# Issuing three opening loads from ScalarE behind its statistics, and spreading the loads of x, in an attention and gated-MLP kernel

## The chip, the cores and the metric

The kernel runs on one core of one Trainium2 chip. The metric is the device time of one execution in microseconds (us), lower is better. A timed execution is some 1.8 us longer than the span of its profile, which runs from the first to the last recorded instruction. A difference of 2% would be 39 us.

## The reference, cut to what matters

```python
xn  = layernorm(x)                                    # x: 2048 x 640, bfloat16
q   = xn @ wq                                         # 32 heads of 192
p   = softmax(q k_cache^T * 192**-0.5)                # 2048 keys per head
s   = (p @ v_cache, heads side by side) @ wo
g   = silu((silu(xn @ w1) * (xn @ w3)) @ w2)          # hidden size 1536
out = x + s * g
```

## The kernel before: the parts that the change touches

The kernel goes through the 32 heads, each with four blocks of 512 queries. TensorE's program is a fixed list: scores, values and projections, interleaved. The opening has to bring head 0 and query block 0 to the point where that list can run. Loads are issued by SyncE (`nc.sync`), weights by GpSimd (`nc.gpsimd`). Cut to the core:

```python
def head_start():
    load_x(0, 0, 2)              # x of query block 0, in two parts
    load_x(0, 2, 4)
    load_k0(0)                   # K of head 0, keys 0..1023 ("K half 0")
    load_w0()                    # three weight loads, issued by GpSimd
    load_k0(1)                   # K half 1
    load_x(1)                    # x of block 1 ("x1")
    load_v(0, (0,))              # V half 0
    turn_over(34)                # 34 matmuls on the identity: warm-up of TensorE
    ln_stats(0, 0)               # layernorm statistics: VectorE
    ln_stats(0, 1)
    ln_stats_act(0, 3)           # ... and ScalarE, for one tile
    ...
    turn_k0(pk0, 0, range(4))            # TensorE transposes K half 0 (16 of them)
    copy_k0(nc.scalar.copy, pk0, 0, 0)   # ScalarE copies K^T out of PSUM
    turn_over(4)
    ln_turn(0, 0, nc.scalar.copy)        # x^T, first half: TensorE, then ScalarE's copy
    turn_k0(pk1, 1, (0, 1))              # K half 1
    ln_turn(0, 1, nc.vector.tensor_copy) # x^T, second half, VectorE's copy
    ...
    load_v(0, (1,))
    for g in range(2, NQB):              # x of blocks 2 and 3
        load_x(g)
    project_first()                      # the first query projection
    ...
    ln_norm(1, 0, nc.vector)
    ln_norm(1, 1, nc.vector)
    ln_turn_dma(1, 0)                    # x^T of block 1: two DMA transposes, SyncE
    ln_turn_dma(1, 1)
    ln_stats(1, 3)
```

In the profile, L271 is the transposes of K, L391 the first query projection, L410 the second one (block 1, which needs the two DMA transposes), L569 the warm-up, `kn` the landing place of K of head 0, `W` the weights, `pst` the transposes of x.

## Time and profile before

| | before |
|---|---|
| median of the first three runs | 1942.58 us (1942.23 to 1942.89) |
| the profiled execution | 1944.41 us timed, span 1942.6 us |
| PE busy | 1930.4 us, 99% |
| idle of PE, largest | 2.8 (identity), 2.4 (K half 0), 0.7 (x^T of block 1) |

From the profile page of the kernel before: busy time, share of the span and instruction count of each engine, then the chain of work that ended last, by engine.

```profile
PE 1930.4 (99%) x27267; PEld 1319.7 (68%) x27275; DVE 654.3 (34%) x997; ACT 1180.5 (61%) x1278; POOL 282.5 (15%) x501
...
PE 98%; DMA 1%; DVE 1%; ACT 0%; issue 0%; SPq 0%; DVEq 0%; ACTq 0%
```

TensorE bounds the kernel, and only its idle time can be won. The waits of PE in the kernel before (waiting instruction and what released it: us in total, times, longest) show all of it:

```profile
PE pk L569 <- POOL ident_bf masks.py:199: 2.8, 1, 2.8
PE pk L271 <- DMA kn<-in_A_k_cache_dram: 2.4, 1, 2.4
PE ps L410 <- DMA xnT<-xn: 0.7, 1, 0.7
PE ps L391 <- ACT xnT L356: 0.3, 1, 0.3
PE st L487 <- ACT pT L490: 0.3, 1, 0.3
```

The timeline of PE in the kernel before (start in us, length in us, instruction, count, and in brackets the idle time before it with its releaser):

```profile
8.94 1.89 PE L271 MATMUL pk<-ident_bf,kn 128*128 128x128 bf16 x16 [2.35 <-DMA kn<-in_A_k_cache_dram]
...
13.54 2.34 PE L391 MATMUL ps<-xnT,W 128*128 128x256 bf16 x20 [0.31 <-ACT xnT L356]
...
29.02 2.32 PE L410 MATMUL ps<-xnT,W 128*128 128x512 bf16 x9 [0.66 <-DMA xnT<-xn]
```

K half 0 lands and PE transposes it at 8.94; 16 transposes take 1.89 us, one each 107 ns. That is half clock: in later parts of this trace the same transposes start 56 ns apart. The chain of waits gives the transfers' lengths (start, us, what): K half 0 was issued at 1.68 and took 7.21 us; the DMA transpose that released L410 was issued at 22.80 and took 6.09 us.

```profile
1.68 7.21 DMA kn<-in_A_k_cache_dram
...
22.80 6.09 DMA xnT<-xn
```

The weights' issues in the first 5 us, from the transfer view (size, us from issue to landing). They were issued at 1.30, 2.66 and 3.55, so they landed at 8.7, 11.1 and 13.0:

```profile
W<-in_A_wq_dram POOLq DMA_DIRECT2D x1, 160.0 KB, 7.4
W<-in_B_w_dram POOLq DMA_DIRECT2D x1, 80.0 KB, 8.4
W<-in_A_wq_dram POOLq DMA_DIRECT2D x1, 80.0 KB, 9.4
```

### The profile page before, as it was taken

The numbers are of one execution on the slowest core, as the hardware profiler recorded it, in microseconds if no ns is written. First come the engines' busy times: TensorE is split into PE (matmuls) and PEld (weight loads), VectorE is DVE, ScalarE is ACT, GpSimd is POOL, SyncE is SP. The second block draws the span as 40 slices with busy tenths as digits, with TensorE's granted clock in tenths as the row PEclk, the third lists the DMA queues.
The fourth block names the chain that finished last, engine by engine and source line by source line (L and its number), as shares of the span: only waits on it lengthen the run. The fifth ranks groups of instructions, "written<-read, shape, count | busy, mean of one in ns | idle before, by whom it ended". The sixth has DMA issues, their size and how long they took to land.

```text
span 1942.6 us, 59661 instructions
## 1 busy us (share of the span) xinstructions
PE 1930.4 (99%) x27267; PEld 1319.7 (68%) x27275; DVE 654.3 (34%) x997; ACT 1180.5 (61%) x1278; POOL 282.5 (15%) x501
## 2 busy tenths in 40 slices
PE   8999999999999999999999999999999999999998
PEld 5666666666666666666666666666666666577776
DVE  6433333333333333333333333333333334521111
ACT  5667776767676767676777677677767677210000
POOL 2111111111111111111111111111111110000000
PEclk9999999999999999999999999999999999999999
DMA  7743433323243434353434343434334220937882
GB/s 173 135 97 69 92 77 65 94 59 90 55 98 66 95 66 101 68 161 68 98 67 101 68 100 68 97 68 99 70 64 91 63 73 2 258 67 137 153 153 60
DMA packets 394643, 178.98 MB, mean 92 GB/s; under 512 B 341616, under 2 KB 382832, under 8 KB 394384
## 3 DMA queue, kind: packets, MB, share of 16 engines
q1 hardware_dynamic: 372464, 126.76, 30.8%
q0 software_dynamic: 19472, 45.71, 9.8%
q8 instruction: 215, 3.52, 0.8%
q10 hardware_dynamic: 2448, 2.62, 0.5%
q14 instruction: 44, 0.36, 0.1%
HBM read 52.82 MB, written 27.79 MB: 41 GB/s over the span
## 4 chain that ended last, share of the span: by engine, by line
PE 98%; DMA 1%; DVE 1%; ACT 0%; issue 0%; SPq 0%; DVEq 0%; ACTq 0%
PE obank L516 35%; PE st L487 33%; PE ps L424 14%; PE ps_s L111 11%; PE ps_f L727 3%; PE ps_gu L701 1%; PE st L488 1%; DMA kn<-in_A_k_cache_dram 0%; PE ps L410 0%; DMA xnT<-xn 0%; DVE stats L316 0%; PE ps L391 0%; PE pk L271 0%; ACT xnT L356 0%; DVE xn L346 0%
## 5 line engine op out<-in xcount | busy, mean ns | idle before, releaser
L490 ACT ACTIVATE pT<-st 128x1024 bf16<-128x1024 f32 x1024 | 1046.3, 1022 | 251.7 <-PE st L488 235.7
L516 PEld LDWEIGHTS <-pT 64*128 64x128 bf16 x16384 | 713.9, 94 | 241.8 <-ACT pT L490 0.2
L516 PE MATMUL obank<-vt,pT 64*128 64x193 bf16 x16384 | 851.9, 243 | 0.0
L487 PE MATMUL st<-qC,KW 64*128 64x512 bf16 x2046 | 605.8, 376 | 0.1
L525 DVE COPY osum<-obank 128x772 f32<-128x772 f32 x128 | 123.2, 962 | 788.9 <-PE obank L516 788.9
L488 PE MATMUL st<-qB,KW 64*128 64x512 bf16 x1024 | 385.2, 376 | 0.0
L487 PE MATMUL st<-qA,KW 64*128 64x512 bf16 x1022 | 384.5, 376 | 0.4 <-ACT pT L490 0.3
L488 PE MATMUL st<-qC,KW 64*128 64x512 bf16 x1022 | 384.5, 376 | 0.0
L488 PE MATMUL st<-qA,KW 64*128 64x512 bf16 x1022 | 384.4, 376 | 0.0
L487 PEld LDWEIGHTS <-KW 64*128 64x128 bf16 x3068 | 278.1, 94 | 153.6 <-issue 2.1
L424 PE MATMUL ps<-xnT,W 64*128 64x512 bf16 x1280 | 297.2, 376 | 0.0
L424 PE MATMUL ps<-xnS,W 64*128 64x512 bf16 x1280 | 296.3, 376 | 0.0
L488 PEld LDWEIGHTS <-KW 64*128 64x128 bf16 x3068 | 278.4, 94 | 0.7 <-issue 0.6
L377 POOL DMA_DIRECT2D qC<-qA x124 | 65.4, 528 | 1285.7 <-DVE rl_all L532 1270.1
L430 ACT CAST qB<-ps 128x512 bf16<-128x512 f32 x131 | 76.7, 585 | 229.2 <-PE ps L424 222.9
L111 PE MATMUL ps_s<-wo_sb,oT 128*128 128x384 bf16 (+3 forms) x1535 | 208.8, 299 | 0.1
L424 PEld LDWEIGHTS <-W 64*128 64x128 bf16 x2560 | 123.0, 94 | 121.1
L111 PEld LDWEIGHTS <-oT 128*128 128x128 bf16 x1536 | 148.3, 98 | 60.5
L526 DVE TENSOR_TENSOR osum<-osum,obank 128x772 f32<-128x772 f32 x128 | 122.7, 959 | 13.4
L533 DVE TENSOR_TENSOR ostage<-osum,rl_all 128x768 bf16<-128x768 f32 x128 | 122.6, 958 | 4.4
L465 DVE SCALAR_TENSOR_TENSOR hT<-pt,qB 64x512 bf16<-64x512 bf16 x64 | 43.7, 683 | 199.5 <-ACT pt L464 199.5
L429 DVE CAST qA<-ps 128x512 bf16<-128x512 f32 x131 | 90.6, 692 | 25.6 <-PE ps L410 7.8
(84 smaller groups left out, 625.4 us busy)
## 6 DMA issues: line engine op xcount, KB each, us to landing
vt<-in_A_v_cache_dram SPq DMA_DIRECT2D x64, 384.0 KB, 5.6
o_scr<-ostage SPq DMA_DIRECT2D x16, 1536.0 KB, 10.2
qC<-qA POOLq DMA_DIRECT2D x248, 64.0 KB, 1.9
qC<-qB POOLq DMA_DIRECT2D x124, 64.0 KB, 2.3
wo_sb<-in_A_wo_dram POOLq DMA_DIRECT2D x1, 7680.0 KB, 35.9
W<-in_A_wq_dram POOLq DMA_DIRECT2D x32, 160.0 KB, 3.3
W<-in_B_w_dram POOLq DMA_DIRECT2D x32, 80.0 KB, 3.2
W<-in_A_wq_dram POOLq DMA_DIRECT2D x32, 80.0 KB, 2.9
```

The costliest lines, as they stand in the source:

```text
L111: nc.tensor.matmul(ps[:, 0:w], lhsT=oT[:, k, :], rhs=wo_sb[:, k, c0:c1], start=(k == 0), stop=(k == OC - 1))
L377: nc.gpsimd.dma_start(out=qC[0:64, half, :], in_=qAB[half][64:P, :])
L424: nc.tensor.matmul(ps[:, r * 512:(r + 1) * 512], lhsT=W[rows, j, :], rhs=xs[rows, j // 2, qs], start=(j == 0), stop=(j == 2 * DC - 1))
L429: a = nc.vector.tensor_copy(out=qAB[0][:], in_=ps[:, 0:512])
L430: b = nc.scalar.copy(out=qAB[1][:], in_=ps[:, 512:1024])
L487: nc.tensor.matmul(st2[:, 0:512], lhsT=ka, rhs=qa, start=r == 0 and nr == 3, stop=r == nr - 1)
L488: nc.tensor.matmul(st2[:, 512:1024], lhsT=kb, rhs=qb2, start=r == 0 and nr == 3, stop=r == nr - 1)
L490: nc.scalar.activation(out=pT2[:], in_=st2[:], func=ACT.Exp, scale=att_scale)
L516: nc.tensor.matmul(obanks[r][:, j * 256:j * 256 + DH + 1], lhsT=pT2[r * 64:(r + 1) * 64, t * 512 + j * P:t * 512 + (j + 1) * P], rhs=vt[r ...
L525: nc.vector.tensor_copy(out=osum[:], in_=ov[0])
L526: nc.vector.tensor_tensor(out=osum[:], in0=osum[:], in1=ov[1], op=ALU.add)
L533: nc.vector.tensor_tensor(out=ostage[:, qb * 4:qb * 4 + 4, hg * DH:(hg + 1) * DH], in0=osum[:, :, 0:DH], in1=rl.unsqueeze(2).to_broadcast( ...
```

## The change

The first loads of head 0 (x0, K half 0, weights) are to have the DMA engines to themselves. K half 1, x1 and V half 0, which are needed later ("far" loads), are issued by ScalarE behind its two statistics passes. x of block 2 stays in its place, x of block 3 ("x3") goes behind the two DMA transposes of block 1, out of their way.

```diff
@@ head_start
-        load_k0(0)
+        load_k0(0, nc.sync)
         load_w0()
-        load_k0(1)
-        load_x(1)
-        load_v(0, (0,))
         turn_over(34)
         ln_stats(0, 0)
         ln_stats(0, 1)
         ln_stats_act(0, 3)
+        load_k0(1, nc.scalar)
+        load_x(1, queue=nc.scalar)
+        load_v(0, (0,), nc.scalar)
         ln_stats(0, 2)
 ...
         load_v(0, (1,))
-        for g in range(2, NQB):
-            load_x(g)
+        load_x(2)
         project_first()
 ...
         ln_turn_dma(1, 1)
+        for g in range(3, NQB):
+            load_x(g)
         ln_stats(1, 3)
```

(The helpers get a `queue` argument; nothing else differs, and TensorE's and VectorE's programs are the same.)

More of the change, by code (lines that the diff above doesn't have):

```diff
@@ L211, in _kernel_impl, with load_x @@
     loads = {}
-    def load_x(g, t0=0, t1=4):
-        nc.sync.dma_start(out=x_sb[:, 4 * g + t0:4 * g + t1, :],
+    def load_x(g, t0=0, t1=4, queue=nc.sync):
+        queue.dma_start(out=x_sb[:, 4 * g + t0:4 * g + t1, :],
                           in_=x2[g * 512:(g + 1) * 512, :].rearrange("(p t) d -> p t d", t=4)[:, t0:t1, :])
@@ L258, in _kernel_impl, with load_k0 @@
     HP = NPAIR // 2
-    def load_k0(half):
+    def load_k0(half, queue):
         if half == 0:
@@ L264, in load_k0 @@
             loads.setdefault(0, {}).update(KW=kvp.tile([P, 5, HK], BF16, tag="KW", name="KW"))
-        nc.sync.dma_start(out=k0["v"][:, half * HP:(half + 1) * HP, :].rearrange("p j c -> p (j c)"),
+        queue.dma_start(out=k0["v"][:, half * HP:(half + 1) * HP, :].rearrange("p j c -> p (j c)"),
                           in_=A_k_cache[0, 0, half * HK:(half + 1) * HK, :].rearrange("(p t) d -> p (t d)", p=P))
@@ L281, in shift_k0, with load_v @@
         nc.vector.tensor_copy(out=KW[0:64, 3, :], in_=KW[64:P, 0, :])
-    def load_v(h, halves=(0, 1)):
+    def load_v(h, halves=(0, 1), queue=nc.sync):
         vt = vts[h % 2]
@@ L288, in load_v @@
             if h == 0:
-                nc.sync.dma_start(out=vt[:, t * NPAIR:(t + 1) * NPAIR, 0:DH],
+                queue.dma_start(out=vt[:, t * NPAIR:(t + 1) * NPAIR, 0:DH],
                                   in_=A_v_cache[0, h, t * HK:(t + 1) * HK, :].rearrange("(i s) d -> i s d", i=P))
```

## The prediction

> **What bounds the kernel now.** TensorE. The page gives PE 1930.4 of 1942.6 us busy (99%), and the chain of waits is 98% PE. From about 18 us its stream is nearly gapless, so time can only be gained in the opening. The waits view lists PE's idle: 2.8 us for the identity, 2.4 us for the first half of K of head 0, 0.7 us for a transposed block of x, 0.3 and 0.3. The change touches the second and third: at most some 3.4 us, 0.18%. The verdict is "within 2%" either way.
>
> **How the opening runs (timeline, transfers).** SyncE issues six loads back to back, 0.75 to 3.8 us: x0 (two parts, landed 3.56 and 4.41), K half 0 (issued 1.68, landed 8.89), K half 1 (9.70), x1 (13.2), V half 0 (15.8). GpSimd's weights, issued 1.3 to 4.4, land 8.73, 11.07 and 12.98. PE's 34 warm-up matmuls end at 6.58; it idles 2.35 us until K lands and turns K at half clock (107 ns per 128 columns; the clock record goes from 0.5 to 1 at 12.0 us). The chain goes on through ACT's copy of x^T to the first projection at 13.54, the weights landing only 0.5 us before.
>
> **What the change does.** K half 1, x1 and V half 0 go to ScalarE behind its two statistics passes (4.43 to 6.2 us). Three issues should cost it about 0.34 + 0.34 + 0.65 us (its stores took 0.34; V's issue 0.69 on SyncE), where it idles 4.65 us: free. Only x0, K half 0 and the weights then share the DMA engines up to about 6.5 us. K half 0 already precedes the others in its ring, so the gain is less sharing: 328 to 369 GB/s flow between 6 and 9 us, much of it K half 1 and x1. The Trainium skill (DMA: Bandwidth & Descriptors, Queues, rings and completion order) says that each DMA engine alternates between rings packet by packet; the trace fits: weight packets begin right after a ring finishes K half 0, then alternate with it. So the weights should land earlier too, about 8.5 to 10.
>
> Estimate: K half 0 at 6.6 to 7.8 instead of 8.89, so PE's gap shrinks by 1.1 to 2.3. The opening moves with it, if K half 1 lands by about 10 (I expect 8.5 to 10).
>
> x3 moves behind the two DMA transposes of block 1. They were issued at 21.4 and 22.8 and landed at 26.7 and 28.9, behind x2 and x3 (24.1, 25.9); later ones land 2.6 to 3.5 us after issue. They should land by 26.5, which removes PE's 0.66 us wait before the second query projection: 0.4 to 0.7 us.
>
> If PE's gap gets short enough, the clock may reach full speed one 3.4 us window earlier (the skill, TensorE: Matmul & The Clock Gate, Part 1); PE 70% busy in the 3.4 us before 5.2 us did not do it. Up to 0.5 us. Against: K half 1 or V late, or ScalarE held up, −0.5.
>
> **Prediction.** Gain 2.1 us: 1940.5 us, 8 in 10 between 1938.9 and 1942.2. Faster by over 2%: 0.003; within 2%: 0.994; slower: 0.003.
>
> **What would show it.** First K transpose near 7; three DMA issues on ScalarE between 5.3 and 7.9; weights landed before 11; first projection 1 to 2.5 us before 13.54; PE's wait on transposed x gone; PE busy otherwise unchanged. **Wrong if** K half 0 still lands after 8.3 (its slowness between 4 and 6 us, where only 150 GB/s flow, may not come from the loads behind it), or PE gets a new wait on K half 1, the weights or V.

## The result, and the profile after

| | before | changed |
|---|---|---|
| median at the time of the prediction, six runs each | 1942.51 us | 1941.88 us |
| range | 1942.23 to 1942.93 | 1941.22 to 1942.74 |
| profiled execution: timed, span | 1944.41, 1942.6 us | 1941.37, 1939.6 us |
| all runs, mean | 1943.00 us (38 runs) | 1941.56 us (16 runs) |

The ratio was 0.9997, with a 95% interval of 0.9984 to 1.001. Ratios here are the mean time of one kernel's runs over that of the other's of the same rounds, so they are not quite the ratio of the medians. In three sessions the mean of the changed kernel lay 0.65, 1.98 and 1.59 us below that of the kernel before. The recorded interval of each session includes 1, so it is the agreement of the three that speaks for a small gain, about 1.4 us or 0.07%, against runs of one kernel that differ among themselves by 2 to 3 us.

The two profiles differ by 3.0 us of span, far more than the medians. First the page of the changed kernel, answering the lines shown above:

```profile
PE 1928.9 (99%) x27267; PEld 1317.8 (68%) x27275; DVE 654.2 (34%) x997; ACT 1181.2 (61%) x1278; POOL 282.6 (15%) x501
...
PE 98%; DVE 1%; DMA 0%; ACT 0%; issue 0%; SPq 0%; POOL 0%; DVEq 0%; ACTq 0%
```

The waits of PE in the changed kernel: the wait for K half 0 shrank from 2.4 to 1.3, the one on x^T of block 1 is gone.

```profile
PE pk L569 <- POOL ident_bf masks.py:199: 2.8, 1, 2.8
PE pk L271 <- DMA kn<-in_A_k_cache_dram: 1.3, 1, 1.3
PE ps L391 <- ACT xnT L356: 0.4, 1, 0.4
PE st L487 <- ACT pT L490: 0.3, 1, 0.3
```

The timeline of PE in the changed kernel. The first projection starts 2.34 us earlier. But K landed only 1.04 us earlier; the other 1.3 us come from the transposes and the few matmuls among them, which run at full clock here (16 transposes in 1.07 us):

```profile
7.90 1.07 PE L271 MATMUL pk<-ident_bf,kn 128*128 128x128 bf16 x16 [1.32 <-DMA kn<-in_A_k_cache_dram]
...
11.20 2.34 PE L391 MATMUL ps<-xnT,W 128*128 128x256 bf16 x20 [0.44 <-ACT xnT L356]
...
25.94 2.33 PE L410 MATMUL ps<-xnT,W 128*128 128x512 bf16 x9
```

ScalarE's timeline in the changed kernel (ACTq is its sequencer issuing a load). The issues run beside the second statistics pass, not after it, and are over at 6.77; ScalarE's next work, L277, comes at 9.00:

```profile
5.24 0.83 ACT L339 ACTIVATE xn<-x_all,mv 128x640 bf16<-128x640 bf16 x1
5.24 0.39 ACTq L265 DMA_DIRECT2D kn<-in_A_k_cache_dram  x1
5.67 0.45 ACTq L214 DMA_DIRECT2D x_all<-in_A_x_dram  x1
5.97 0.19 ACT L339 ACTIVATION_READ_ACCUMULATOR xn<-x_all,mv 128x1 f32 x1
6.15 0.62 ACTq L289 DMA_DIRECT2D vt<-in_A_v_cache_dram  x1
9.00 1.01 ACT L277 COPY KW<-pk 128x1024 bf16<-128x1024 bf16 x1 [2.85 <-PE pk L271]
```

The weights of the changed kernel, issued at 1.30, 2.67 and 3.56, all land by 8.3 us, up to 4.7 us earlier than before:

```profile
W<-in_A_wq_dram POOLq DMA_DIRECT2D x1, 160.0 KB, 6.1
W<-in_B_w_dram POOLq DMA_DIRECT2D x1, 80.0 KB, 5.4
W<-in_A_wq_dram POOLq DMA_DIRECT2D x1, 80.0 KB, 4.7
```

### The profile page after: what moved, and what is told of

Its sections match the earlier page's. It is cut to its first block, busy times and chain, and to the rows that moved or that the text cites. A ratio compares the mean times of both kernels' runs of the same rounds, so it can differ in the third digit from the quotient of the medians.

```text
span 1939.6 us, 59659 instructions
## 1 busy us (share of the span) xinstructions
PE 1928.9 (99%) x27267; PEld 1317.8 (68%) x27275; DVE 654.2 (34%) x997; ACT 1181.2 (61%) x1278; POOL 282.6 (15%) x501
## 4 chain that ended last, share of the span: by engine, by line
PE 98%; DVE 1%; DMA 0%; ACT 0%; issue 0%; SPq 0%; POOL 0%; DVEq 0%; ACTq 0%
PE obank L516 35%; PE st L487 33%; PE ps L424 14%; PE ps_s L111 11%; PE ps_f L728 3%; PE ps_gu L702 1%; PE st L488 1%; PE ps L410 0%; DMA kn<-in_A_k_cache_dram 0%; DVE stats L316 0%; PE ps L391 0%; DVE xn L346 0%; DVE mv L317 0%; DVE qA L429 0%; ACT xnT L356 0%
## 5 line engine op out<-in xcount | busy, mean ns | idle before, releaser
L526 DVE TENSOR_TENSOR osum<-osum,obank 128x772 f32<-128x772 f32 x128 | 122.7, 958 | 13.4
```

Source lines behind the costliest of these rows:

```text
L526: nc.vector.tensor_tensor(out=osum[:], in0=osum[:], in1=ov[1], op=ALU.add)
```

## The experiments

Three questions: why do two profiles differ by 3 us and the medians by 0.6; what is each part of the change worth; and is it the issuing engine or the moment of issue that helps. Twelve experiments were run (three of them repeat one of the two kernels), five timed runs each, four at a time on the same chip. Theory A says that each execution has its own luck with the TensorE clock; theory B that only the transfers vary. Theory F says that the moment of issue matters; rival G that the second issuing engine does.

This table, read from the fourteen traces, is used throughout. "Rest" is the span less the start of the first projection: what the kernel needs from there to the end. "Clock" is when the trace's clock record first has full speed.

| run | far loads issued | x3 | clock | K half 0 landed | last weights landed | first projection | span | rest |
|---|---|---|---|---|---|---|---|---|
| before (first profile) | SyncE, 2.2 to 3.8 | early | 12.0 | 8.89 | 12.98 | 13.54 | 1942.65 | 1929.1 |
| e0_before | SyncE | early | 14.3 | 8.23 | 12.00 | 13.37 | 1942.40 | 1929.0 |
| e2_act_only | ScalarE, 5.5 to 7.0 | early | 10.8 | 7.61 | 8.04 | 12.29 | 1941.80 | 1929.5 |
| e3_x3_only | SyncE | late | 11.1 | 7.52 | 11.30 | 12.26 | 1940.86 | 1928.6 |
| changed (first profile) | ScalarE | late | 6.7 | 7.85 | 8.28 | 11.20 | 1939.60 | 1928.4 |
| e1_after | ScalarE | late | 11.3 | 7.35 | 8.16 | 12.09 | 1940.51 | 1928.4 |
| e4_after | ScalarE | late | 6.9 | 7.39 | 8.16 | 10.73 | 1939.05 | 1928.3 |
| w_before | SyncE | early | 6.5 | 8.32 | 12.12 | 11.66 | 1941.69 | 1930.0 |
| w_x3 | SyncE | late | 5.9 | 7.68 | 12.59 | 11.03 | 1941.49 | 1930.5 |
| w_after | ScalarE | late | 5.3 | 6.93 | 8.18 | 11.37 | 1940.63 | 1929.3 |
| w_best | ScalarE | late | 4.5 | 7.58 | 8.05 | 11.27 | 1939.66 | 1928.4 |
| v_best | ScalarE | late | 10.4 | 7.31 | 7.89 | 11.63 | 1940.08 | 1928.5 |
| e5_act_early | ScalarE, first of all | late | 6.8 | 11.12 | 11.07 | 16.26 | 1945.16 | 1928.9 |
| e6_sync_late | SyncE, from 5.9 | late | 6.8 | 7.53 | 7.92 | 17.15 | 1947.17 | 1930.0 |

### First set: both kernels again, and each half of the change

**e0_before**: no edit.

> The kernel before, unchanged, against itself. Its first profile was of an execution of 1944.41 us, 1.9 us above the 1942.5 us of its six timed runs, so that profile may not be typical. Theory A (clock phase): each execution falls in one of two cases, the TensorE clock reaching full speed at about 6.7 us or at about 12 us; 1942.5 is the early case, 1944.4 the late one. Then a profile of an execution of 1942.5 us shows the first 16 K transposes taking about 1.1 us, not 1.89, and the first projection at 11.5 to 12.2 us, not 13.54. Theory B (transfers): the fast and slow executions differ in when K half 0 lands (8.89 in the slow one), with the transposes at 107 ns in both. Ratio 1.000.

Measured: 1942.13, 1942.29, 1943.29, 1944.17 and 1944.37 us. The profiled execution is the one of 1944.17, with a late clock (14.3 us). So the spread is in the kernel itself, and the expected case (early clock in a profile of a 1942.5 us execution) was not caught. Here the half clock lasted into the first projection, which took 2.81 us instead of 2.34:

```profile
13.37 2.81 PE L391 MATMUL ps<-xnT,W 128*128 128x256 bf16 x20
```

**e1_after** and, in the third set, **e4_after**: the changed kernel, no edit.

> The changed kernel again. Its six runs fell in two groups, 1941.2 to 1941.4 and 1942.4 to 1942.7. Theory A: the same two groups again, 1.1 us apart, and the page shows an early clock (first 16 K transposes 1.08 us) if the profiled execution is of the lower group, a late clock (about 1.9 us) if of the upper. Theory B: groups differ by when K half 0 lands. Median 1941.2 to 1942.6, ratio 0.9993 to 0.9998.

> The changed kernel once more, beside the three below on the same chip. From its eleven timed runs so far: 1940.8 to 1942.8, median 1941.2 to 1941.9; 0.5 to 2 us below the kernel before. K half 0 at 6.9 to 7.9 (so far 7.85, 7.35; kernels with all loads on SyncE 7.5 to 8.9), weights at 8.0 to 8.3.

Measured: e1_after 1940.79, 1941.04, 1941.10, 1942.28, 1942.57 (two groups as at first, the median 1941.10 just below the expected range); e4_after 1940.78 to 1941.43. The profiled executions were those of 1942.28 and 1940.82 us, one of each group. The timeline of PE in the slower one, e1_after:

```profile
7.39 1.89 PE L271 MATMUL pk<-ident_bf,kn 128*128 128x128 bf16 x16 [0.81 <-DMA kn<-in_A_k_cache_dram]
...
12.09 2.34 PE L391 MATMUL ps<-xnT,W 128*128 128x256 bf16 x20
```

and in the faster one, e4_after:

```profile
7.44 1.07 PE L271 MATMUL pk<-ident_bf,kn 128*128 128x128 bf16 x16 [0.86 <-DMA kn<-in_A_k_cache_dram]
...
10.73 2.34 PE L391 MATMUL ps<-xnT,W 128*128 128x256 bf16 x20 [0.40 <-ACT xnT L356]
```

Same program, K half 0 landed within 0.05 us of the same moment, and yet the first projection starts 1.36 us earlier in e4_after, because its transposes run at 56 and not at 107 ns. The spans differ by 1.46 us. This is the clearest pair: theory A holds for the changed kernel in all three of its traces (early clock: 1941.37 and 1940.82 us; late: 1942.28). Theory B is not empty, as K half 0 lands at different times in different executions (the table), but it can't explain this pair. And the early clock is no merit of the change: it came at 6.7 and 6.9 us, before K half 0 had landed, when PE had run nothing but the 34 warm-up matmuls that both kernels have. No trace of the kernel before with its own warm-up happened to show an early clock, so that it has such executions too is likely (the switch precedes anything that differs), not shown.

The fourteen traces also show what decides the draw. The switches of the clock record lie 3.41 us or twice that apart (6.78, 10.19 and 17.02 us in e5_act_early; 6.83, 13.66 and 20.48 in e6_sync_late), so each trace has a grid of windows of 3.41 us. In every one the clock went to full speed at the end of the first window in which PE was busy for about 90% (0.90) or more; windows with 77% or less never did it. In e4_after the warm-up, 2.77 to 6.58 us, fills 3.12 us of the window that ends at 6.87. In e1_after a window ends at 7.91, only 2.61 us of it are busy, and the switch comes at the end of the next. Where the grid lies differs from execution to execution. As the warm-up is only 0.4 us longer than a window, it fills one well enough in between a third and some 55% of all positions (an estimate from these lengths, with 90% and 77% as the two limits); it did so in four of the nine traces with this warm-up.

**e2_act_only**: the changed kernel, with x3 put back.

```diff
-        load_x(2)
+        for g in range(2, NQB):
+            load_x(g)
 ...
-        for g in range(3, NQB):
-            load_x(g)
         ln_stats(1, 3)
```

> Only the loads issued by ScalarE; x of block 3 stays where it was. Theory A and my prediction: K half 0 at 7.6 to 8.1, weights by 9, first projection as in the changed kernel, but TensorE then waits on the second DMA transpose of block 1 before the second query projection, which gives back 0.5 to 2 us: 1941.8 to 1943. Rival C: the move of x3 matters nothing, and this equals the changed kernel in both groups (1941.3 and 1942.5).

**e3_x3_only**: the kernel before, with only x3 moved (the same lines the other way).

> Only the move of x of block 3; all loads on SyncE. Predicted: TensorE's 0.66 us wait before the second query projection goes, so 0.4 to 0.7 us below before in either clock case: 1941.9 (early clock), 1943.8 (late). Rival C: no difference (1942.5 or 1944.4). First K transposes and first projection as in the kernel before.

Measured, means: e2_act_only 1942.27, e3_x3_only 1941.69, both together (e1_after) 1941.56, the kernel before of the same rounds 1943.54 us. So e3_x3_only gained 1.9 us where 0.4 to 0.7 were expected; part of that cannot be the move, as its trace has K half 0 at 7.52, before anything that was moved is issued. The second query projection in e2_act_only, from the timeline of PE:

```profile
28.19 2.32 PE L410 MATMUL ps<-xnT,W 128*128 128x512 bf16 x9 [0.76 <-DVE ve L319]
```

and in e3_x3_only, where it waits for nothing:

```profile
27.00 2.33 PE L410 MATMUL ps<-xnT,W 128*128 128x512 bf16 x9
```

(The releaser named, DVE, had long been done; the two DMA transposes of e2_act_only took 6.5 and 7.2 us from issue to landing, the last landing at 28.06, and those of e3_x3_only 2.9 and 4.4.) So ScalarE's part alone starts the projection earlier and gives some of it back at the next transfer: its rest is 1929.5, against 1928.4 with x3 moved. In the table, the rest is 1929.0 to 1930.0 in all four traces with x3 early. With x3 late it is 1928.3 to 1928.6 in six of eight; the other two, w_x3 and w_after, have a new wait, see below (e5_act_early and e6_sync_late, which spoil the opening in other ways, are left out). But not all of that difference is the work of x3. PE waits for the second DMA transpose in three of the four traces with x3 early (0.7 us in the first profile, 0.8 in e2_act_only, 0.5 in w_before) and in none of the ten with x3 late. In e0_before it does not wait:

```profile
28.59 2.33 PE L410 MATMUL ps<-xnT,W 128*128 128x512 bf16 x9
```

There the transpose landed at 27.50, and 0.5 of the 0.6 us by which its rest is longer are what its first projection lost to the half clock. Most of the remaining excess of e2_act_only and w_before is another wait of PE (0.5 and 0.8 us). So the move removes a wait of 0.5 to 0.8 us from the executions that have it. It is the best-founded part of the gain. Rival C, that the move matters nothing, falls. What ScalarE's part adds in time is not resolved in this set: 0.1 us beside e3_x3_only, where K half 0 happened to land at 7.52 although SyncE had issued everything at once.

### Second set: take the luck of the clock away

The four kernels start the warm-up at 1.07 us, on a tile that VectorE sets, and make it longer, so that PE is busy long enough before K lands.

```diff
+    wt = const.tile([P, P], BF16, name="wt")
+    nc.vector.memset(wt[:], 1.0)
 ...
-    def turn_over(k):
+    def turn_over(k, src=ident_bf):
         for i in range(k):
-            nc.tensor.matmul(warm, lhsT=ident_bf[:], rhs=ident_bf[:], start=True, stop=True)
+            nc.tensor.matmul(warm, lhsT=src[:], rhs=src[:], start=True, stop=True)
 ...
-        turn_over(34)
+        turn_over(60, wt)
```

w_before, w_x3 and w_after are the kernel before, e3_x3_only and the changed kernel with this edit. w_best also drops `turn_over(4)` and lets ScalarE copy x^T before K^T:

```diff
-        copy_k0(nc.scalar.copy, pk0, 0, 0)
-        turn_over(4)
         ln_turn(0, 0, nc.scalar.copy)
+        copy_k0(nc.scalar.copy, pk0, 0, 0)
```

> The kernel before, with its 34 warm-up matmuls (started at 2.77 us, on the identity) replaced by 60 on a tile that VectorE sets at 0.8 us. TensorE is then busy from about 1.1 us, so the clock should be at full speed before K half 0 lands in every execution. Theory A (clock phase and K's landing spread the times; the weights limit behind them): first 16 K transposes about 1.1 us; first projection then starts when the third weight load lands, 11.3 to 13 us, not when x^T is copied; the times spread by under 1 us and the median is 0.5 to 1.5 us below before. Theory D (the clock is not what spreads the times): no change in median, spread of 2 us stays.

> The same warm-up with only the move of x of block 3. Theory A: first projection held by the weights (11.3 to 13 us), no wait before the second query projection: 0.5 to 1 us below the kernel before with this warm-up, and 0.5 to 1.3 us above the changed kernel with it. Rival E: equal to the changed kernel with it.

> The same warm-up in the changed kernel. Theory A: always the early-clock case: transposes 1.1 us, weights at 8 to 8.5, first projection 10.7 to 11.4 us, 1940.8 to 1941.5 us in all five runs, and 1.2 to 2 us below the kernel before with the same warm-up, as here the weights' landing (8 against 11.3 to 13 us) counts. Rival E (ScalarE's issue is worth nothing): equal to the next kernel, with the x3 move alone.

> The changed kernel with the same warm-up, and ScalarE copies the first half of x^T before its first copy of K^T (the four filler matmuls between are dropped). With weights at 8.3 us the first projection waits for ScalarE, which copies K^T for 1.0 us first: it should start about 0.9 us earlier, at about 10 to 10.4, and the end 0.5 to 0.9 us earlier than the changed kernel with the warm-up: 1940.0 to 1940.8. If ScalarE's copies of K^T then hold up the first scores, the gain is lost there.

Measured, medians: w_before 1942.53 (1942.26 to 1944.23), w_x3 1942.45, w_after 1942.29, w_best 1941.64 (1941.51 to 1941.87), the kernel before of the same rounds 1942.91 us. The clock was early in all four traces (4.5 to 6.5 us), as wanted. But the means are only −0.3 (w_x3), −0.8 (w_after) and −1.2 us (w_best) from the kernel before, w_before gains nothing (+0.1), and its spread did not shrink. Most of the expectation failed, and the waits tell why. Those of PE in w_before:

```profile
PE pst L356 <- DVE qA L431: 0.8, 1, 0.8
PE ps L412 <- DVE mv L319: 0.5, 1, 0.5
```

The early clock brought its first projection to 11.66 instead of 13.4 to 13.5, and then PE lost 1.4 us again, some 14 us later. VectorE stood 0.85 us at its statistics of block 2, whose x landed at 23.55, and what stood behind it in its program came 0.8 us late; the other 0.5 us are the wait for the second DMA transpose, which landed at 27.88 (the releaser named is again not the last). w_x3 and w_after have the same wait of 0.8 us. An opening that runs ahead can meet the next landing; it need not, as e4_after started its first projection earlier still (10.73), had x of block 2 at 21.1 and no such wait. In w_x3 the wait that the expectation asked for is there:

```profile
PE ps L393 <- DMA W<-in_A_wq_dram: 1.0, 1, 1.0
```

With SyncE issuing all loads at once the last weights land at 12.59 us, and an opening with an early clock waits 1.0 us for them here (in w_before, with the last weights at 12.12, they were just in time). With the far loads late they are there at 8.2 and no such wait exists. So the early weights, the surest effect of ScalarE's issue, can be worth something only in executions whose clock is early; in those with a late clock the first projection comes too late to notice. In time w_x3 is 0.5 us slower than w_after in the mean, in the expected direction, within the noise.

w_after and w_best had a fault of mine: as I read it, their builds gave the first projection another of the two PSUM buffers (TensorE's result memory), so that it waited for VectorE's copy of the second half of x^T:

```profile
PE ps L393 <- DVE xnT L358: 1.0, 1, 1.0
```

That line is from the waits of PE in w_best. w_after and w_best are therefore no clean test of the early warm-up.

### Third set: which engine, or when

**e5_act_early**: the changed kernel with the three far loads as ScalarE's first instructions.

```diff
         load_w0()
+        load_k0(1, nc.scalar)
+        load_x(1, queue=nc.scalar)
+        load_v(0, (0,), nc.scalar)
         turn_over(34)
 ...
         ln_stats_act(0, 3)
-        load_k0(1, nc.scalar)
-        load_x(1, queue=nc.scalar)
-        load_v(0, (0,), nc.scalar)
```

> The same three loads on ScalarE, but as its first instructions, ahead of its statistics instead of behind. Theory F (when they are issued counts[...]): they now share the engines with x0 and K half 0 from about 2 us, so x0 lands later than 4.6, K half 0 later than 8.5, the weights later than 9.5, and the time is 1 to 3 us above the changed kernel. Rival G (a second issuing engine is what helps): landings and time as in the changed kernel.

Measured: 1946.31 us median (1945.72 to 1946.93), 3.5 us above the kernel before and 5.1 above the changed one (means), more than the 1 to 3 expected. From the chain of waits of e5_act_early:

```profile
1.68 9.44 DMA kn<-in_A_k_cache_dram
```

K half 0 took 9.44 us instead of the 5.7 to 6.2 of the changed kernel, because x1 and K half 1 shared the DMA engines with it from the start (K half 1, needed last, landed first, at 5.6 us). G falls for this: a second issuing engine alone does not help, and opened this early it does harm. The Trainium skill (DMA: Bandwidth & Descriptors, Issuing engines are not separate DMA queues) says that loads started by different engines run on the same 16 DMA engines and interleave; this run shows it, and that interleaving costs the load that is needed first. The long gap also lost the clock. Stretches of e5_act_early (stretch, length, busy time and instructions of PE, PEld, DVE, ACT and POOL, then PEclk, DMA share, GB/s):

```profile
8.00:10.00 2.00, 0.00 (x0) 0.00 (x0) 1.25 (x4) 1.64 (x4) 0.59 (x1) 1.00 1.12 242
10.00:12.00 2.00, 0.83 (x9) 0.84 (x10) 1.63 (x5) 0.11 (x2) 1.63 (x2) 0.55 0.59 132
```

In a gap of 4.6 us without a matmul, which began at 6.6, PEclk goes from 1.00 to 0.50 at 10.2; it is back at 17.0 us.

**e6_sync_late**: the same loads on SyncE, but behind a 512-byte store of a column that ScalarE's first pass writes, so that SyncE issues them as late as ScalarE would. The store's result is used by nobody.

```diff
+    dly = dram.tile([P, 1], F32, name="dly")
 ...
-        load_k0(1, nc.scalar)
-        load_x(1, queue=nc.scalar)
-        load_v(0, (0,), nc.scalar)
+        nc.sync.dma_start(out=dly[:], in_=lnorm[0][0][:, 3, 0:1])
+        load_k0(1, nc.sync)
+        load_x(1)
+        load_v(0, (0,))
```

> The same three loads on SyncE, as late as ScalarE issues them: SyncE first stores a column that ScalarE's first statistics pass writes (512 bytes to a scratch, used by nobody), so it issues them from about 5.3 us. Theory F: as in the changed kernel, K half 0 at 6.9 to 7.9, weights at 8 to 9, time within 0.7 us of it. Rival G: landings as in the kernel before (weights 11 to 13), time 0.5 us or more above the changed kernel.

Measured: 1948.94 us, 6.2 us above the kernel before, so as a kernel it fails, for a reason that I had not foreseen. Transfers of e6_sync_late issued between 5 and 8 us:

```profile
kn<-in_A_k_cache_dram SPq DMA_DIRECT2D x1, 384.0 KB, 9.3
...
dly<-mv SPq DMA_DIRECT2D x1, 0.5 KB, 7.3
```

The store of 512 bytes in 4-byte pieces took 7.3 us to land, K half 1 behind it in the same queue landed at 15.2 us, and PE waited 5.8 us for that. But what it was built for can be read all the same: K half 0 at 7.53 and the weights at 7.9 us, as in the changed kernel, with SyncE issuing. With e5_act_early this settles the weights: keep the far loads back, on either engine, and they land at about 8; issue them early, from either, and they land at 11 to 13. Theory F holds for the landings; its forecast of the time failed. The swap of engines is not a like-for-like one, as the store kept the far loads back beyond their issue: between 7.5 and 9.0 us nothing flowed (0 GB/s, against 365 in the changed kernel). What it shows is that no second engine is needed. ScalarE is only a convenient place for a late issue, since its program reaches it at 5.2 us without an artificial wait.

**v_best**: w_best with 46 warm-up matmuls instead of 60, which gives back the intended PSUM buffer.

```diff
-        turn_over(60, wt)
+        turn_over(46, wt)
```

> The kernel with the early warm-up and ScalarE's copy of x^T first, with 46 warm-up matmuls instead of 60. With 60 its build gave the first projection the PSUM buffer that VectorE frees last (its matmul waited for that copy, till 11.27 us); with 46 it gets the one that ScalarE frees. Expected: first projection at 10.2 to 10.9 us, clock early in most executions, 1940.2 to 1941.3 us, spread under 1 us, 0.3 to 1 us below the changed kernel. If the wait for VectorE's copy was not what held it, 1941.6 as before.

Measured: 1941.16 us median (1940.45 to 1943.28); the changed kernel of the same rounds 1941.32 (1940.78 to 1941.43). The wait for VectorE's copy is gone (the first projection waits 0.2 us, for ScalarE), but the clock of the profiled execution was late (10.4 us): five us of warm-up were not enough there, and the first projection came at 11.63, not at the expected 10.2 to 10.9. The spread, 2.8 us, is not the expected one of under 1 us either. No version here beats the changed kernel by more than the noise. w_best has the narrowest times, 0.36 us, and is no faster.

## Why the prediction was right or wrong, point by point

The range held, at first by 0.3 us (1941.88 against an upper end of 1942.2), and "within 2%" was never in doubt. It was wide, a gain of 0.3 to 3.6 us, and so it held the 0.65 to 1.98 us of all three sessions. The first two profiles, 3.0 us apart, would have seemed to confirm more than the predicted 2.1; but 1.3 us of that is the draw of the clock, which is luck. The point, a gain of 2.1 us, was 1.5 us more than the 0.63 us measured at first, and 0.7 more than the 1.4 us of all runs.

- **"K half 0 at 6.6 to 7.8 instead of 8.89, so PE's gap shrinks by 1.1 to 2.3."** This is the mis-sized term. The new landing was about right: 6.9 to 7.9 us in eight traces with late far loads, mean 7.4. The old one was not: 8.89 came from an execution 1.9 us longer than the median. Five traces with early far loads have 7.52 to 8.89, mean 8.1. So K comes 0.7 us earlier on average, and as the two ranges overlap, even that is likely rather than settled. The numbers to see this stood beside the profile: 1944.41 us for its execution, 1942.6 for the timed runs. The reason given, less sharing, is shown for the weights; for K in the kernel before it is not. The stretch that the prediction doubted is where the traces differ: between 4 and 6 us the five with all loads early on SyncE move 153, 227, 216, 247 and 291 GB/s, with K at 8.89, 8.23, 8.32, 7.68 and 7.52, and the eight with late far loads 284 to 340. So in these five K comes late where little flows in all, and why little flows stays open.
- **"The weights should land earlier too, about 8.5 to 10."** They landed at 7.9 to 8.3. That they share the engines with the far loads is shown by e5_act_early and e6_sync_late. But the prediction let them count for the start of the first projection in any execution; they can limit only where the clock is early (1.0 us in w_x3, nothing in w_before).
- **"The clock may reach full speed one window earlier ... up to 0.5 us."** The size was 1.4 us, and the cause was wrong: the early switch preceded K half 0, so the shorter gap did not make it. It is a draw in each execution, decided by where the windows fall. The predicted effect exists too: in e0_before K landed at 8.23, the window from 7.49 to 10.90 was 77% busy, and full speed came a window later, at 14.3; the first projection lost 0.5 us by it. (The sentence that the clock record goes from 0.5 to 1 at 12.0 us was also inexact: the record begins there, and the stretches before show 1.00; the half clock is read from the 107 ns of a transpose.)
- **x3: "removes PE's 0.66 us wait ... 0.4 to 0.7 us", transposes "by 26.5".** Right in kind: the second transpose landed at 25.0 and the wait is gone in every trace of the changed kernel. In size, the wait was 0.5 to 0.8 us in three of four traces with x3 early, about as forecast, and absent in the fourth.
- **"Three issues ... free", K half 1 "8.5 to 10", "no new wait".** Right: 5.24 to 6.77 us in idle time of ScalarE, K half 1 at 9.2 us, no new wait of PE in the changed kernel.

What stays open: how the 1.4 us divide between the two halves of the change (e2_act_only and e3_x3_only gained 1.3 and 1.9, the two together 2.0 in the same rounds, each with an uncertainty of some 0.7 us, an estimate from the 0.7 us standard deviation of single runs), and why K half 0 of the same program lands anywhere between 7.5 and 8.9 us.

## What to carry to other kernels

Before costing a change from one profile, compare the time of the profiled execution with the median of the timed ones: here the difference of the two was as large as the whole gain in question. Loads that are needed late should be issued late, from whichever engine gets there without waiting; a second queue opened early takes bandwidth from the first. And when an opening is shortened, look up the landings 10 to 20 us further on, since the time can be given back at the first of them that did not move.

## What the Trainium skill lacked or had wrong

- TensorE: Matmul & The Clock Gate, Part 1, places full speed around 4 us of sustained matmuls, give or take 0.5 us. Here a warm-up of 3.8 us (34 matmuls from 2.77 us) followed by a gap gave full speed at 6.7 to 6.9 us in some executions and at 10.8 to 14.3 us in others of nearly the same opening. The page's free-running window fits that, and it warns that runs differ by it; what it lacks is how busy a window must be (90% was enough in every trace here, 77% or less in none) and that a warm-up just longer than the window is a draw worth 1.4 us. A warm-up of five us (46 matmuls from 1.06 us) missed it too in the one execution traced (10.4 us); 60 made it in four of four (4.5 to 6.5 us).
- A point where the page held: it says that the clock is lost after an idle window of some 3.4 us and regained after a busy one. Both agree with e5_act_early: PE ran nothing from 6.6 to 11.2 us and had half clock from 10.2 us. It came back at 17.0 us, 5.8 us after the matmuls had resumed, which fits the windows: the one up to 13.6 us was only 71% busy, the next one was full.
- DMA: Bandwidth & Descriptors warns of small descriptors, but has no figure for a tiny store ahead of loads in the same queue: 512 bytes in 4-byte pieces took 7.3 us to land, and the 384 KB load behind it 9.3 us from its issue, against 3.7 to 4.0 us on ScalarE's queue in the changed kernel.
- Perfetto Trace Analysis does not tell the reader to check whether the traced execution is typical; here two traces of the same program differ by 1.46 us of span (e1_after, e4_after).
